# A causal convolution and a SiLU block on one core: the output weights' combinations on VectorE, and another order for the first blocks

## The chip, the cores and the metric

The kernel runs on one core of a Trainium2 chip. The metric is the device time of one execution in microseconds (us), lower is better. The profile and the trace come from one profiled execution; the runs' times come from executions of their own.

## The reference

What is computed, cut to what matters (all in float32):

```python
# x: (8, 4096, 192), weight: (8, 7), w_in: (192, 2048), w_out: (2048, 192)
w = exp(weight - max(weight, axis=-1)); w = w / (sum(w, axis=-1) + 1e-9)
x_pad = concatenate([zeros(B, 6, D), x], axis=1)
y[b, s, c] = sum over k of w[head(c), k] * x_pad[b, s + k, c]      # causal, 7 taps, 24 channels per head
h = y.reshape(32768, 192) @ w_in
g = h * (1 / (1 + exp(-h)))
out = g @ w_out
```

## The kernel before

**Work in blocks.** The 32768 tokens are cut into 32 blocks of 1024, and a block into two halves of 512. Channels are cut into 3 pieces of 64, the 2048 hidden units into 4 groups of 4 x 128. For each block the kernel loads x (SP's queue, line 289), transposes it (DVE, line 548), convolves it (first tap on ACT, line 579; six taps on DVE, line 582), copies pieces of the result to slots (DMAs on SP's queue, line 599), multiplies up to h (TensorE, called PE), takes SiLU (ACT), and multiplies down (PE) to the output, which is transposed (DVE, line 838) and stored (SP's queue, line 848).

**Fewer products.** From block 1 on, the up and down multiplications are written as bilinear schemes with fewer products. The up products of a block are 20 per group, 80 in all (line 656, two matmul records each). They take combinations of the convolved pieces (the *windows*, DVE, line 607) and combinations of the weights w_in, which are made once, in place, by `combine`: groups 0 and 1 on POOL, groups 2 and 3 on VectorE (DVE). The down multiplication takes sums of g (DVE, line 711) and combinations of w_out, made once by `combine_out`, in the tiles wx and, in place, wo. Block 0 is multiplied plainly, both ways: up at line 634, down at line 765. So wo may be combined only once block 0's plain down steps have read it, group by group.

**The order is written out by hand.** Every engine works through its own instructions in program order, and the program order of the loop is a list of tokens. `step(b, token)` (line 865) issues one token. A prefix says which block is meant: none is b, `-` is b-1, `=` is b-2, `+` is b+1. START (line 91) is run once with b = 2 and covers block 0's plain down steps, blocks 1 and 2, and block 3 up to its last up products and about half its output slots; PLAN (line 65) is then run for b = 3, 4, ... and begins with the rest of block b. The tokens that matter here:

- `ld.k`: four loads of x for the next block (SP's queue); `i.k`: the transpose of that piece; `ha.0`: the six columns ahead of the block
- `v.ki`: tap i of piece k, for the next block; `v.k0` is on ACT and `v.k1` to `v.k6` on DVE, each adding to the one before it. With `=` they make block 1's
- `sp.n`: one copy of a convolved piece to a slot (SP's queue), a piece's as soon as its six taps are in; `w.n`: a window. `w.3` and `w.4` need `sp.2`, `sp.3`, `sp.5` and `sp.6`, and `w.5` needs `w.4` and `sp.1`
- `Pn.g`: an up product of group g. The first, `P7.0`, reads window 4; `P1` and `P8` read window 5. `k12.0` copies a bank on DVE before `P2.0` may add to it. Other names with h, i, j, k, u or S are copies, sums and SiLU between products, on DVE and ACT
- `t.jk`: a sum of g for group j (DVE); `Di.je`: an output slot's four column-tiled matmuls (line 746). D2.30 needs t.30 and t.31, D5.30 needs t.33
- `M`, `z`, `y`, `x`: the merge of the output slots; `o.n`: a transpose of the merged output (DVE); `st.n`: its stores (SP's queue)
- `dp.n`: one of 48 plain down steps of block 0 (four matmul records at line 765), group j's last one being dp.11, dp.23, dp.35 and dp.47; `cp.n`: its copies out (ACT, line 783)
- `go.n`: half of the combination of w_in for groups 2 and 3, on DVE: go.0 and go.1 (7 and 6 operations) for one half of the rows, go.2 and go.3 (8 and 7) for the other, all of 64 x 256

SP's queue is also in program order: a store that waits for its transpose holds back the loads behind it.

**What the change touches.** `combine_out(j)` (line 488) makes four tensor_tensor operations of 128 x 192 (2 x 96 columns) for group j, through `comb` (line 467) on POOL. It is called for all four groups from the generator `down_plain` (line 755), at its end, right after the last plain step is issued (lines 777 to 779). POOL's earlier work is in its queue ahead of it: the combination of w_in for groups 0 and 1. DVE's work before the loop is the rounding of the weights (`rounded`, line 393).

Of the kernel before, what the change touches and what calls it, by code (L numbers as in the profile page):

```python
# [17 lines left out]
def kernel(  # L18
# [29 lines left out]
    NJ = NM // 2  # L48
# [43 lines left out]
        "=dp.0 =dp.1 =dp.2 =dp.3 =dp.4 =dp.5 =dp.6 =dp.7 =dp.8 =dp.9 =dp.10 =dp.11 =dp.12 =dp.13 "  # L92
        "=dp.14 =dp.15 =dp.16 =dp.17 =dp.18 =dp.19 =dp.20 =dp.21 =dp.22 =dp.23 =dp.24 =dp.25 "
        "=dp.26 =dp.27 =dp.28 =dp.29 =dp.30 =dp.31 =dp.32 =dp.33 =dp.34 =dp.35 =dp.36 =dp.37 "
        "=v.00 =dp.38 -ld.2 =v.01 =dp.39 =v.10 =dp.40 =dp.41 =v.11 =v.20 -ld.1 =v.02 =v.21 =v.03 "
        "=dp.42 =v.12 =dp.43 =v.04 =v.22 =v.13 =v.05 =v.23 =v.24 =dp.44 =v.06 =sp.0 =sp.3 =v.14 "
        "=v.25 =v.15 =sp.2 =dp.45 =v.26 =sp.7 =sp.10 =v.16 =sp.8 =go.2 =go.0 =sp.6 =sp.4 =sp.9 "
        "=w.0 =sp.1 =w.1 =w.2 =dp.46 =sp.5 =w.3 =w.4 -P7.0 =w.5 -P1.0 =cp.0 -P7.1 =cp.1 -P1.1 "
        "=dp.47 -h15.0 =go.1 -k12.1 -P8.0 -h15.1 -P2.1 -P8.1 -k12.0 -P2.0 -h17.1 =cp.2 =go.3 "
        "-P17.1 -u4.0 -P5.0 -P18.1 -k8.0 -j4.0 -ld.0 -h17.0 -u4.1 -P5.1 -S19.1 -j4.1 -k5.0 -i.2 "  # L100
        "-P18.0 =o.2 -P11.0 -u10.0 -P17.0 -P6.0 -P16.0 -k8.1 -P3.0 -P10.0 -P11.1 -h18.0 -i15_f.0 "
        "-P0.0 -P6.1 -u6.0 -P19.0 -k5.1 -S19.0 -P9.0 -j6.0 -P16.1 -k9.0 -P3.1 -u10.1 -P10.1 "
        "-P13.0 -S14.0 -i15_f.1 -u6.1 -P7.2 -h18.1 -S20.0 -P4.0 -j6.1 -P0.1 -P9.1 -P19.1 -k17.0 "
        "-k9.1 -P12.0 -j10.0 -P15.0 -S13.0 -P13.1 -i17_f.0 -S14.1 -i18_10.0 =o.0 -P7.3 -h15.2 "
        "-P4.1 -h15.3 -P8.2 -k17.1 -j10.1 -P1.2 -S20.1 -S13.1 -P14.0 -u4.2 -P12.1 -P8.3 -P1.3 "
        "-i15_11.0 -i17_f.1 -k12.2 -P15.1 -h17.2 -S16.0 -P5.2 -P17.2 -k12.3 -u4.3 -P2.2 -i18_10.1 "
        "-P18.2 -P2.3 -P14.1 -j4.2 -k8.2 =o.1 -P5.3 -i.0 -h17.3 -S15.0 -P17.3 -S19.2 -P11.2 "
        "-P18.3 -k5.2 -P3.2 =st.0 -P16.2 -i15_11.1 -j4.3 -S18.0 -S16.1 -k5.3 -P6.2 -u10.2 -u6.2 "
        "-S19.3 -h18.2 -k8.3 -P16.3 -P3.3 -h18.3 -P10.2 -P9.2 -P0.2 -P6.3 -P19.2 -t.00 -j6.2 "
        "-P11.3 -i15_f.2 -S17.0 -i.1 -u6.3 -k9.2 =st.1 -j6.3 -P19.3 -u10.3 -S14.2 -S20.2 -ha.0 "  # L110
        "-t.01 -P4.2 -k9.3 -P0.3 -P13.2 -S13.2 -t.03 -P10.3 -P13.3 -k17.2 -i15_f.3 -P4.3 -P15.2 "
        "-k17.3 -P9.3 -j10.2 -P15.3 -D0.01 -S13.3 -S14.3 -i18_10.2 -D4.00 -j10.3 -P14.2 -S16.2 "
        "-P12.3 -v.20 -i18_10.3 -P14.3 -ze.0 -P12.2 -S15.1 -t.02 -D4.01 =st.2 -i15_11.2 -D1.11 "
        "-i17_f.2 -S17.2 -D5.00 -D0.00 -D5.01 -D3.00 -D3.01 -i15_11.3 -v.21 -v.10 -S20.3 -v.22 "
        "-S17.1 -t.10 -D2.01 -v.00 -S18.1 -t.11 -t.13 -D0.20 -D2.11 -D2.00 -t.12 -D1.00 -D4.10 "
        "-i17_f.3 -D4.11 -D0.10 -D5.10 -D1.21 -S15.2 -D0.11 -D2.10 -v.23 -D0.21 -S18.2 -D5.11 "
        "-S17.3 -v.11 -D3.10 -S16.3 -D3.11 -D1.20 -S18.3 -t.20 -v.01 -D1.01 -D1.30 -t.21 -v.12 "
        "-D0.30 -v.02 -t.22 -D1.10 -S15.3 -D2.21 -D0.31 -D2.20 -t.23 -D3.20 -D4.20 -D4.21 -v.24 "
        "-v.13 -v.25 -t.30 -v.26 -v.14 -t.31 -sp.7 -D2.31 -D1.31 -y0.0 -z1.0 -v.03 -sp.9 -sp.8 "
        "-D2.30 -v.15 -y2.0 -v.04 -v.16 -D3.21 -v.05 -v.06 -D5.20 -t.33 -t.32 -D5.31 -D5.21 "  # L120
        "-sp.10 -y1.0 -D5.30 -D3.31 -sp.6 -D3.30 -sp.4 -D4.31 -D4.30 -w.0 -sp.2 -sp.0 -sp.5 -w.2 "
        "-sp.1 -w.1 -M1.0 -sp.3 -x0.0 -x2.2 -x2.1 -w.3 -w.4 -x2.0 P7.0 -w.5 -x1.0 ld.1 h15.0 P1.1 "
        "P7.1 -M3.0 P1.0 -x2.3 h15.1 k12.1 h17.1 P8.0 k12.0 u4.0 P2.1 P8.1 P2.0 P17.1 u4.1 -M2.0 "
        "P5.0 P18.1 P5.1 -M4.0 j4.0 -M5.0 k5.0 P16.0 P3.0 k8.0 h17.0 h18.0 S19.1 P18.0 P6.0 P17.0 "
        "u6.0 -M6.0 P11.0 P0.0 k8.1 j6.0 P9.0 P19.0 P11.1 S19.0 u10.0 S14.0 j4.1 P10.0 P6.1 k5.1 "
        "-o.0 P3.1 S20.0 k9.0 P16.1 u10.1 u6.1 -o.1 h18.1 -M7.0 P13.0 P7.2 P4.0 ld.2 P10.1 P9.1 "
        "P0.1 i15_f.0 j6.1 h15.2 i15_f.1 k17.0 P12.0 P19.1 j10.0 -o.2 S13.0 k9.1 P13.1 i17_f.0 "
        "P15.0 S20.1 P4.1 P7.3 S14.1 k17.1 S17.0 P1.2 i18_10.0 j10.1 h15.3 P8.2 S13.1 i.1 P12.1 "
        "P14.0 P1.3 u4.2 P8.3 P5.2 k12.2 P15.1 i15_11.0 P2.2 h17.2 P18.2 -st.0 S16.0 i17_f.1 u4.3 "
        "k12.3 P5.3 P17.2 S15.0 k8.2 i18_10.1 h17.3 -st.1 P11.2 j4.2 P14.1 S19.2 j4.3 P2.3 P18.3 "  # L130
        "ld.0 k5.2 P3.2 P17.3 i15_11.1 u10.2 i.0 u6.2 S18.0 S16.1 P6.2 k5.3 P16.2 P3.3 j6.2 S19.3 "
        "k8.3 P10.2 h18.2 P9.2 P16.3 P11.3 i15_f.2 P19.2 P6.3 P0.2 u6.3 -st.2 k9.2 h18.3 P13.2 "
        "S17.1 S14.2 S20.2 t.00 u10.3 P19.3 j6.3 P4.2 P10.3 -o.3 i.2 t.01 -st.3 ha.0 k9.3 k17.2 "
        "P13.3 S13.2 k17.3 P0.3 P15.2 P9.3 P4.3 t.03 S20.3 P15.3 D1.31 D1.11 D1.01 j10.2 v.00 "
        "S18.1 i15_f.3 S14.3 v.20 j10.3 P12.3 i18_10.2 i18_10.3 P14.2 P12.2 P14.3 ze.0 t.02 v.10 "
        "v.01 D1.21 i17_f.3 S15.1 D5.01 D4.00 D2.01 S16.2 t.10 S18.2 D4.01 D2.00 D5.00 i17_f.2 "
        "t.11 D2.10 D0.00 D0.10 v.11 v.02 D2.11 i15_11.2 S15.2 t.13 v.12 D3.00 D3.01 D1.10 t.12 "
        "D4.11 i15_11.3 D0.21 D5.11 v.03 S17.3 D4.10 D3.11 S18.3 D1.30 S17.2 v.04 D0.01 D0.11 "
        "D1.20 t.20 D0.20 v.21 S15.3 D5.10 t.21 v.22 t.22 v.13 D3.10 D2.21 t.23 v.14 D4.21 D2.20 "
        "D5.21 D0.31 D3.21 v.05 v.23 S13.3 v.24 D4.20 D3.20 S16.3 D1.00 D0.30 z1.0 D5.20 v.15 "  # L140
        "v.25 v.16 v.06 v.26 sp.5 t.30 t.31 D2.30 D2.31 sp.1 t.33 t.32 D3.30 D5.30 D5.31 D4.31 "
        "D3.31 D4.30 sp.8 sp.4 y2.0 sp.7 sp.9 w.0 y0.0 sp.2 sp.0 sp.10 x2.1 w.2 sp.6 w.3 w.1 sp.3 "
        "y1.0 w.4 x0.0 +P7.0 M1.0 x1.0 x2.3 +h15.0 w.5 +P1.1 x2.0 +P7.1 +h15.1 +P1.0 +P8.0 M2.0 "
        "M3.0 +k12.1 +h17.1 +u4.0 +P2.1 +k12.0 x2.2 +P8.1 +P2.0 M4.0 +j4.0 +P18.1 +P5.0 +P17.1 "
        "M5.0 +u4.1 +P5.1 +k5.0 +h17.0 +P16.0 +P3.0 +P18.0 +k8.0 +P6.0 M6.0 +u6.0 +j4.1 +h18.0 "
        "+S19.1 +k8.1 +P17.0 +j6.0 M7.0 +P11.0 +P0.0 +S19.0 +P9.0 o.1 +P19.0 +P11.1 +u10.1 +k5.1 "
        "+P16.1 +P3.1 +u10.0 +S20.0 +k9.0 +P10.0 +i15_f.0 +h18.1 +P6.1 +P10.1 +u6.1 +P13.0 +P19.1 "
        "+P4.0 +P0.1 +S14.0 +k17.0 +S13.0 +P9.1 +j6.1 +P7.2 +P12.0 +k9.1 +i15_f.1 +j10.0 +P15.0 "
        "+P1.2 +S20.1 +P7.3 +h15.2 +S14.1 +i17_f.0 +P13.1 +P8.2 +P4.1 +k12.2 +k17.1 +i18_10.0 "
        "+h15.3 +j10.1 +P14.0 +S17.0 +S13.1 +u4.2 +P2.2 +P8.3 +P12.1 +i15_11.0 +P15.1 +h17.2 "  # L150
        "+i17_f.1 +P5.2 +i18_10.1 +u4.3 +P17.2 +P1.3 +S15.0 +k12.3 +S16.0 +P18.2 +P5.3 +P14.1 "
        "+j4.3 +k8.2 +h17.3 st.1 +P11.2 +P18.3 +P2.3 +S19.2 +S16.1 +P17.3 +j4.2 +i15_11.1 +k5.2 "
        "+P6.2 +u10.2 +P16.2 +k5.3 +P3.2 +P16.3 +u6.2 +S19.3 +P3.3 +j6.2 +P10.2 +k8.3 +h18.2 "
        "+P6.3 +i15_f.2 +u6.3 +P19.2 +h18.3 +j6.3 +P9.2 +S18.0 +P0.2 +P11.3 +P0.3 +k9.2 +P4.2 "
        "+P19.3 +S14.2 +S20.2 +P13.2 +u10.3 +k9.3 +P10.3 +P13.3 +S13.2 +t.00 +S18.1 +S20.3 +k17.2 "
        "+D1.00 +P15.2 +P4.3 +t.01 +i15_f.3 +k17.3 +P15.3 +P12.3 +D1.11 +D0.00 +D1.31 +D0.01 "
        "+t.03 +j10.3 +S13.3 +t.02 o.2 +D4.01 +i17_f.3 +D3.00 +j10.2 +i18_10.3 +P9.3 +i18_10.2 "
        "+P14.2 +P12.2 +P14.3 +D1.21 +i17_f.2 +D3.01 +S15.1 +S17.2 o.3 +D4.00 +ze.0 +S17.1 +D5.00 "
        "+S16.2 +D0.20 +S17.3 +i15_11.2 +D5.01 +D2.01 +D2.00 +i15_11.3 st.3 +D1.01 o.0 st.0 "
        "+S18.2 +S15.2 +D1.10 +S15.3 +t.10 +D0.10 +D1.20 +D0.31 +t.11 st.2 +D0.11 +S18.3 +t.13 "  # L160
        "+D2.10 +D4.10 +D5.11 +D2.11 +D1.30 +D0.30 +t.20 +t.21 +D2.21 +D2.20 +D0.21 +S14.3 +D4.11 "
        "+S16.3"
# [592 lines left out]
    def down_plain(b):  # L755

        cmbs[b] = [xpool.tile([P, 4, TB], F32, tag="cmb", name="cmb")]
        for j in range(NJ):
            for a in range(2):
                for e in range(2):  # L760
                    for k in range(NK):
# [12 lines left out]
                        if (a, e, k) == (1, 1, NK - 1):  # L774
                            for c in range(2):
                                del gs[b, j, c]
                            if j == NJ - 1:
                                for c in range(NJ):
                                    combine_out(c)
# [344 lines left out]
```

## Time and profile before

| | us |
|---|---|
| median of 3 runs (lowest to highest) | 2352.57 (2352.14 to 2353.25) |
| the profiled execution's own time | 2355.45 |
| span of its trace | 2353.7 |
| PE busy in the span | 2329.8 (99%) |
| DVE busy | 2180.5 (93%) |
| ACT busy | 1329.0 (56%) |
| POOL busy | 70.0 (3%) |
| DMA, the largest queue (q1), share of 16 engines over the span | 23.1% |

A row of a group in the profile reads: line, engine, operation, output tile <- input tiles, shape, count, then busy time and the mean duration of one in ns, then the idle time of that engine just before such instructions, and what ended it. "L257" is a helper's line that issues every operation of the pinned vector, scalar and POOL engines that has no line of its own. A row of the chain reads: start, duration, and the engine, tile and line whose work the end of the program goes back to. A row of a table of stretches reads: the stretch, its length, and each engine's busy time with the number of instructions, then the granted clock of PE, the DMA engines' busy share and GB/s. PE's records overlap, so its busy time hides small gaps.

### The profile page before, as it was taken

Reading aid. Unit: us, or ns where it says so; the run is one execution under the profiler, and the core shown is the slowest. Engines: PE = TensorE matmul, PEld = TensorE weight load, DVE = VectorE, ACT = ScalarE, POOL = GpSimd, SP = SyncE. Lnnn points to the kernel's source line nnn. Section 1 sums busy time; section 2 is a strip of 40 time slices with the busy share of each in tenths; the row PEclk is TensorE's granted clock in tenths of the full one; section 3 lists DMA queues with packets and bytes.
Section 4 is the critical chain, followed back from the end, with each engine's and each line's share of the span. In section 5 each row is a group of like instructions: output and inputs, shape, how many; then the busy total and the mean of one; then the engine's idle time right before and its main releaser. Section 6 shows DMA issues by size and latency. Waiting matters only on the chain.

```text
span 2353.7 us, 43777 instructions
## 1 busy us (share of the span) xinstructions
PE 2329.8 (99%) x17382; PEld 919.1 (39%) x17382; DVE 2180.5 (93%) x3029; ACT 1329.0 (56%) x2523; POOL 70.0 (3%) x100
## 2 busy tenths in 40 slices
PE   9999989999999999999999999999999999999998
PEld 4344423344333443333443333433334433334433
DVE  8999889999999999999999999999999999999996
ACT  5256535666555765556665457654557655566654
POOL 4500000000000000000000000000000000000000
PEclk9999989999999999999999999999999999999999
DMA  7212122122122222121221221221222221212211
GB/s 157 52 31 36 29 53 49 28 52 52 33 46 45 35 52 48 34 49 30 51 52 37 42 51 30 53 51 30 49 34 47 52 43 40 49 28 52 53 32 23
DMA packets 451245, 106.55 MB, mean 45 GB/s; under 512 B 423584, under 2 KB 428704, under 8 KB 451040
## 3 DMA queue, kind: packets, MB, share of 16 engines
q1 hardware_dynamic: 447392, 101.78, 23.1%
q8 instruction: 136, 2.23, 0.4%
q0 software_dynamic: 448, 1.58, 0.3%
q10 hardware_dynamic: 3200, 0.39, 0.1%
q14 instruction: 69, 0.57, 0.1%
HBM read 31.46 MB, written 25.17 MB: 24 GB/s over the span
## 4 chain that ended last, share of the span: by engine, by line
PE 93%; DVE 2%; SPq 0%; issue 0%; ACT 0%; DMA 0%; ACTq 0%; DVEq 0%
PE ps L746 47%; PE ps L656 46%; DVE nat L582 1%; DVE t L711 0%; SPq L289 0%; DVE w_own L257 0%; DVE g L694 0%; SPq L848 0%; DVE w_other L257 0%; DMA nat<-in_x_dram 0%; DVE ps L694 0%; PE ps L765 0%; DVE u L678 0%; ACT g L691 0%; DVE cmb L257 0%
## 5 line engine op out<-in xcount | busy, mean ns | idle before, releaser
L656 PE MATMUL ps<-win,w_own 64*128 64x512 f32 x1488 | 660.5, 599 | 5.5 <-DVE win L607 5.5
L746 PE MATMUL ps<-g,wo 128*32 128x512 f32 x2976 | 663.6, 593 | 0.0
L746 PE MATMUL ps<-t,wo 128*32 128x512 f32 (+1 forms) x4528 | 512.1, 448 | 0.0
L746 PE MATMUL ps<-t,wx 128*32 128x512 f32 x2976 | 487.5, 595 | 10.9 <-DVE t L711 10.9
L656 PE MATMUL ps<-dup,w_own 64*128 64x512 f32 x1240 | 494.9, 594 | 0.2 <-ACT ps L689 0.2
L691 ACT ACTIVATE g<-ps 128x512 f32<-128x512 f32 x620 | 366.5, 599 | 189.8 <-DVE g L694 112.3
L656 PE MATMUL ps<-dup,w_other 64*128 64x512 f32 x1240 | 457.6, 595 | 0.2 <-ACT ps L689 0.2
L656 PE MATMUL ps<-win,w_other 64*128 64x512 f32 x992 | 446.9, 597 | 0.0
L694 DVE TENSOR_TENSOR g<-g,ps 128x512 f32<-128x512 f32 x496 | 331.6, 684 | 60.9 <-PE ps L656 40.1
L582 DVE SCALAR_TENSOR_TENSOR nat<-xt,turned,nat 128x512 f32<-128x512 f32 x558 | 383.1, 753 | 3.2 <-ACT nat L579 1.1
L811 ACT COPY yx<-ps 32x512 f32<-32x512 f32 x150 | 84.3, 579 | 508.8 <-PE ps L746 507.1
L656 PEld LDWEIGHTS ps<-win,w_own 64*128 64x128 f32 x1488 | 246.6, 186 | 213.7 <-issue 127.5
L711 DVE TENSOR_TENSOR t<-g,t 128x1024 f32<-128x1024 f32 x248 | 302.7, 1221 | 19.4 <-PE ps L746 9.5
L711 DVE TENSOR_TENSOR t<-g 128x1024 f32<-128x1024 f32 x248 | 300.9, 1214 | 12.7 <-PE ps L746 12.7
L746 PEld LDWEIGHTS ps<-t,wo 128*32 128x32 f32 x4528 | 175.7, 110 | 247.9 <-issue 189.4
L694 DVE TENSOR_TENSOR ps<-u,ps 128x512 f32<-128x512 f32 x372 | 255.2, 687 | 13.3 <-PE ps L656 6.1
L656 PEld LDWEIGHTS ps<-dup,w_own 64*128 64x128 f32 x1240 | 195.5, 186 | 144.3 <-issue 78.2
L746 PE MATMUL ps<-g,wx 128*32 128x512 f32 x1488 | 245.6, 592 | 0.0
L691 ACT ACTIVATE g<-g 128x512 f32<-128x512 f32 x372 | 220.5, 625 | 32.5 <-DVE g L694 29.2
L689 ACT ACTIVATE ps<-ps 128x512 f32<-128x512 f32 x372 | 214.7, 584 | 38.1 <-DVE ps L694 19.9
L746 PEld LDWEIGHTS ps<-g,wo 128*32 128x32 f32 x2976 | 172.9, 110 | 146.4 <-issue 145.4
L656 PEld LDWEIGHTS ps<-dup,w_other 64*128 64x128 f32 x1240 | 167.2, 186 | 132.8 <-ACT ps L689 50.7
(102 smaller groups left out, 1838.3 us busy)
## 6 DMA issues: line engine op xcount, KB each, us to landing
dup<-nat SPq DMA_DIRECT2D x221, 128.0 KB, 2.3
nat<-in_x_dram SPq DMA_DIRECT2D x382, 64.0 KB, 2.4
out_dram<-t SPq DMA_DIRECT2D x372, 64.0 KB, 2.0
win<-nat SPq DMA_DIRECT2D x124, 128.0 KB, 2.4
raw<-in_moe_w_out_dram SPq DMA_DIRECT2D x8, 384.0 KB, 3.6
raw<-in_moe_w_in_dram SPq DMA_DIRECT2D x12, 192.0 KB, 5.0
w_other<-w_own POOLq DMA_DIRECT2D x8, 192.0 KB, 5.0
raw<-in_moe_w_in_dram SPq DMA_DIRECT2D x6, 128.0 KB, 3.1
```

What stands on the lines that cost most here:

```text
L582: nc.vector.scalar_tensor_tensor(out=dst, in0=src, scalar=tap, in1=dst, op0=ALU.mult, op1=ALU.add)
L656: nc.tensor.matmul(at(b, "bank", to, g), raw(g, w, e), rows(slot_of(b, x_), e), start=first, stop=True, skip_group_check=True,)
L689: pin(nc.scalar.activation(seen[to], seen[u], AF.Copy, scale=-1.0))
L691: pin(nc.scalar.activation(seen[to], seen[u], AF.Silu, scale=float(sign)))
L694: pin(nc.vector.tensor_tensor(seen[to], seen[u], seen[v], op=op))
L711: pin(nc.vector.tensor_tensor(t[i // 2][:, i % 2, :], u, v, op=ALU.subtract))
L746: nc.tensor.matmul(acc[SQ * q : SQ * q + SQ, to], lhs[:, e, SQ * k : SQ * k + SQ], rhs[:, e, ts(q, TB // 4) if i == 5 else to], start=firs ...
L811: pin(nc.scalar.copy(to, acc(3 * (name[0] == "x") + k)[n:P, :]))
```

## The change

`combine_out` issues its four operations on DVE instead of POOL, and is no longer called from the end of `down_plain`. A new token, `co.j`, calls it for one group. START becomes another order of the same tokens, with the four `=co` added; PLAN is unchanged. No other instruction is added or left out.

```diff
     START = (
-        "=dp.0 =dp.1 =dp.2 =dp.3 =dp.4 =dp.5 =dp.6 =dp.7 =dp.8 =dp.9 =dp.10 =dp.11 =dp.12 =dp.13 "
...
-        "=v.00 =dp.38 -ld.2 =v.01 =dp.39 =v.10 =dp.40 =dp.41 =v.11 =v.20 -ld.1 =v.02 =v.21 =v.03 "
-        "=dp.42 =v.12 =dp.43 =v.04 =v.22 =v.13 =v.05 =v.23 =v.24 =dp.44 =v.06 =sp.0 =sp.3 =v.14 "
-        "=v.25 =v.15 =sp.2 =dp.45 =v.26 =sp.7 =sp.10 =v.16 =sp.8 =go.2 =go.0 =sp.6 =sp.4 =sp.9 "
-        "=w.0 =sp.1 =w.1 =w.2 =dp.46 =sp.5 =w.3 =w.4 -P7.0 =w.5 -P1.0 =cp.0 -P7.1 =cp.1 -P1.1 "
-        "=dp.47 -h15.0 =go.1 -k12.1 -P8.0 -h15.1 -P2.1 -P8.1 -k12.0 -P2.0 -h17.1 =cp.2 =go.3 "
...
+        "=v.10 =v.20 =v.11 =v.21 =v.12 =v.22 =v.13 =v.00 =v.23 =v.01 =v.24 =v.02 =dp.0 =v.14 "
+        "=v.03 =v.25 =v.04 =v.26 =sp.7 =dp.1 =sp.10 =v.05 =v.15 =v.06 =sp.8 =v.16 =sp.9 =go.2 "
+        "=sp.4 =sp.2 =w.0 =dp.2 =sp.0 =w.1 =sp.5 =w.2 =go.3 =w.3 =dp.3 =sp.6 =dp.4 =dp.5 =sp.3 "
+        "-ld.0 =dp.6 =dp.7 =dp.8 =w.4 =dp.9 =dp.10 =dp.11 =co.0 =dp.12 =dp.13 =sp.1 =dp.14 =dp.15 "
...
+        "=dp.40 =dp.41 =dp.42 =go.0 =dp.43 =dp.44 =dp.45 =dp.46 =cp.0 -P7.0 =dp.47 -h15.0 -P8.0 "
+        "-P1.1 =cp.1 -P1.0 -u4.0 -P5.0 -P7.1 -k12.0 -k12.1 -k8.0 =o.1 -P2.0 -j4.0 =cp.2 =co.3 "
...
     def combine_out(j):
...
-        comb(x_[0], a_(1, 0), a_(1, 1), ALU.add)
-        comb(x_[1], x_[0], a_(0, 0), ALU.subtract)
-        comb(x_[2], a_(0, 1), x_[1], ALU.subtract)
-        comb(a_(1, 0), a_(0, 0), a_(1, 0), ALU.subtract)
+        vec.tensor_tensor(x_[0], a_(1, 0), a_(1, 1), op=ALU.add)
+        vec.tensor_tensor(x_[1], x_[0], a_(0, 0), op=ALU.subtract)
+        vec.tensor_tensor(x_[2], a_(0, 1), x_[1], op=ALU.subtract)
+        vec.tensor_tensor(a_(1, 0), a_(0, 0), a_(1, 0), op=ALU.subtract)
...
                         if (a, e, k) == (1, 1, NK - 1):
                             for c in range(2):
                                 del gs[b, j, c]
-                            if j == NJ - 1:
-                                for c in range(NJ):
-                                    combine_out(c)
...
+        elif name == "co":
+            combine_out(digits[0])
```

In block 1's part of the new list, the rest of DVE's early work stands so: `=go.1` between `-u10.1` and `-i15_f.1`, `=co.1` behind `-j6.1`, `=co.2` behind `-i15_f.0`. In the part for block 3, its stores and turned outputs now stand among its up products; these are the lines of before, then of after, that hold block 2's four `o` and four `st`:

```diff
-        "+S19.1 +k8.1 +P17.0 +j6.0 M7.0 +P11.0 +P0.0 +S19.0 +P9.0 o.1 +P19.0 +P11.1 +u10.1 +k5.1 "
...
-        "+j4.3 +k8.2 +h17.3 st.1 +P11.2 +P18.3 +P2.3 +S19.2 +S16.1 +P17.3 +j4.2 +i15_11.1 +k5.2 "
...
-        "+t.03 +j10.3 +S13.3 +t.02 o.2 +D4.01 +i17_f.3 +D3.00 +j10.2 +i18_10.3 +P9.3 +i18_10.2 "
-        "+P14.2 +P12.2 +P14.3 +D1.21 +i17_f.2 +D3.01 +S15.1 +S17.2 o.3 +D4.00 +ze.0 +S17.1 +D5.00 "
-        "+S16.2 +D0.20 +S17.3 +i15_11.2 +D5.01 +D2.01 +D2.00 +i15_11.3 st.3 +D1.01 o.0 st.0 "
-        "+S18.2 +S15.2 +D1.10 +S15.3 +t.10 +D0.10 +D1.20 +D0.31 +t.11 st.2 +D0.11 +S18.3 +t.13 "
...
+        "+P10.0 +S19.0 +j6.0 M7.0 +k5.1 +P6.1 o.2 +S14.0 +P16.1 +k9.0 +P3.1 +u10.1 +P10.1 +S20.0 "
+        "+P13.0 o.1 +P7.2 +h18.1 +u6.1 o.0 +i15_f.0 +k17.0 +P4.0 +i15_f.1 +h15.2 +j6.1 +P0.1 "
...
+        "+h17.2 +P8.3 +j10.1 +P5.2 +P15.1 o.3 +i15_11.0 +P2.2 +i17_f.1 +u4.3 +k12.3 +P17.2 +P2.3 "
+        "+P18.2 +i18_10.1 +S16.0 +k8.2 +P11.2 +P14.1 +P5.3 +j4.2 st.0 +S15.0 +t.00 +i15_11.1 "
+        "+h17.3 +S19.2 +P17.3 st.2 +k5.2 +P3.2 +P18.3 +j4.3 +P6.2 +P16.2 +S16.1 +u10.2 +k5.3 "
+        "+P3.3 +P16.3 +u6.2 +S19.3 +P9.2 +P10.2 +j6.2 +h18.2 +P0.2 +k8.3 st.1 +h18.3 +t.02 +P11.3 "
+        "+P6.3 +S14.2 +k9.2 +P19.2 +u6.3 +P19.3 +i15_f.2 +P13.2 +P4.2 +u10.3 +S20.2 +j6.3 +k9.3 "
+        "st.3 +P10.3 +P13.3 +t.01 +k17.2 +S17.0 +P0.3 +i15_f.3 +P4.3 +k17.3 +P15.2 +P15.3 +P12.2 "
...
```

## The prediction

> **What bounds the kernel now.** I read the page's groups first, for which engine is never idle and what it waited for when it was; then the chain of waits in order of time, for where the idle time lies; then a table of stretches; then the instructions around the two places found.
>
> From the page, the groups of TensorE (PE) with idle time worth naming:
>
> ```profile
> L656 PE MATMUL ps<-win,w_own 64*128 64x512 f32 x1488 | 660.5, 599 | 5.5 <-DVE win L607 5.5
> ...
> L746 PE MATMUL ps<-t,wx 128*32 128x512 f32 x2976 | 487.5, 595 | 10.9 <-DVE t L711 10.9
> ```
>
> PE waits 5.5 us once for a window and 10.9 us once for a sum of g, both made by VectorE (DVE), and for nearly nothing else in 2353.7 us. The chain says when; its pieces that start a block's up products are
>
> ```profile
> 106.56 4.41 PE ps L656 x8
> ...
> 182.67 33.37 PE ps L656 x151
> ...
> 254.31 4.63 PE ps L656 x18
> ...
> 332.65 8.45 PE ps L746 x64
> 341.10 33.29 PE ps L656 x151
> ...
> 412.66 33.30 PE ps L656 x151
> ```
>
> Blocks 1 to 5 begin there: they take 76.1, 71.6, 86.8 and 71.6 us. From 341.10 on every block takes 71.56, which is PE's own work: 80 products of 0.44 (160 matmuls in 33.3 + 1.9), 40 output slots of 0.86, 8 short ones of 0.22, in all 71.3. So the steady loop can't give anything, and it is not changed. START, which ends inside block 3, holds all there is to gain. By stretches (columns: PE, PE weight loads, DVE, ACT, POOL busy; granted clock; DMA share; GB/s):
>
> ```profile
> 100.00:120.00 20.00, 14.52 (x51) 6.85 (x49) 16.81 (x36) 7.86 (x14) 0.00 (x0) 0.83 0.19 38
> ...
> 320.00:340.00 20.00, 9.10 (x76) 2.54 (x68) 19.65 (x28) 3.08 (x7) 0.50 (x1) 0.66 0.31 73
> ```
>
> Each stop is paid twice: idle, then the granted clock is low. The trace's clock records put it at half from 105.94 to 112.77 and from 324.40 to 338.05.
>
> **Stop 1, at 101 to 106.6.** PE ends the last plain down step but one at 101.08 and needs window 4. DVE was never idle before it: it ran v until 96.68, go.2 and go.0 until 103.1, then the windows until 106.4. The 18 v (rows of line 582 alone):
>
> ```profile
> 80.28:92.28 12.00, 11.96 (x12) 1.00 0.00 0
> 93.29:96.70 3.41, 3.39 (x6) 1.00 0.45 106
> 317.87:330.13 12.26, 12.19 (x18) 0.77 0.10 23
> ```
>
> and POOL in the first two stretches:
>
> ```profile
> 80.28:92.28 12.00, 11.53 (x13) 1.00 0.00 0
> 93.29:96.70 3.41, 0.00 (x0) 1.00 0.45 106
> ```
>
> While POOL works, a v starts every 1.00 us; once POOL stops, every 0.66, as in block 3 (18 in 12.26). POOL's work there is combine_out.
>
> **Stop 2, at 321.8 to 332.65.** SP's queue, then DVE's, in block 3:
>
> ```profile
> 298.26 6.03 SPq L848 DMA_DIRECT2D out_dram<-t  x9
> 304.33 7.57 SPq L289 DMA_DIRECT2D nat<-in_x_dram  x12
> ...
> ```
>
> ```profile
> 313.86 0.71 DVE L548 STREAM_TRANSPOSE xt<-nat 128x512 f32<-128x512 f32 x1 [1.39 <-DMA nat<-in_x_dram]
> ...
> 317.87 12.26 DVE L582 SCALAR_TENSOR_TENSOR nat<-xt,turned,nat 128x512 f32<-128x512 f32 x18
> ...
> 331.37 1.23 DVE L711 TENSOR_TENSOR t<-g,t 128x1024 f32<-128x1024 f32 x1
> ```
>
> Block 2's turned outputs (o.3, o.0) stand late in START, so nine stores issue at 298.3, the twelve loads behind them end at 311.9, 57.6 us into the block, and DVE's three transposes wait, with the v, t.30 and t.31 behind them. PE's D2.30 needs t.31. In block 4 the twelve loads issue at 363.15 (22 us into the block) and nothing waits.
>
> **The change, part by part.** *POOL loses combine_out (16 operations, 77.6 to 92.8 and 96.9).* The last two rounding operations before the v, 1.34 and 1.23 us, fall to the 0.95 that the same kind took at 37.6 to 40.5 without POOL's arithmetic: 0.7. Thirteen v at 0.66 for 1.00: 4.4. The new first v (v.11) needs ACT's v.10, which three ACT operations from 76.05 cover. So the v end at 96.68 - 5.1 = 91.6. The Trainium skill (SBUF — State Buffer, section "SBUF: two separate sides") says VectorE with two SBUF inputs and GpSimd lock a port pair for a whole instruction; the pace of 1.00, and not 0.66 + 0.7 (POOL's shortest row), shows slowing, not full turns; the sum takes the measured pace.
>
> *The order up to window 4.* Before it DVE has 15 go operations (go.2, go.3 in place of go.2, go.0) and five windows, as now, 9.4 to 9.7 us: window 4 ends at 101.1. The shares it copies are issued as each third of the v ends, the last needed one (sp.3) at about 94.7 behind nine others of 0.6, and lands 2.4 later, well before. P7.0 then starts at 101.25 instead of 106.56: **-5.3**, with PE's own 101.08 late next.
>
> *What DVE owes after it.* co.0 before window 5, go.0 before k12.0, go.1 and co.1 to co.3 among the products. No row has combine_out on DVE. Below: 0.29 (tensor_scalar, 64x256). Above: 0.69 (128x512). I take 0.36, a little under the 0.42 of a 64x256 tensor_tensor, as 192 columns are fewer: 1.45 per co, 5.8 in all (4.6 to 11.0). P7.0 and the last plain step cover 1.3; co.0 and window 5 take 2.1, so PE waits 0.65 for P8.0. Five products (2.2) later P2.0 needs k12.0, behind go.0's 7 x 0.42: a wait of 1.4. From there DVE is full: k12.0 to w.4 of block 1 are 67.4 us of DVE against 72.2 of PE, DVE starting 4.7 behind, and P15.0, P14.0, P13.2 have margins of 0.1 to 0.4; I allow 1.0. Sum 3.0. Today's block 1 loses 76.1 - 71.56 - 0.86 (the last plain step) = 3.7, mostly half clock: **-0.7**. The co operations' own waits (plain steps 11, 23, 35, 47) end by 102.6 and hold nothing up.
>
> *Block 2* (71.64) keeps its work and slack: 0. Its loads and stores issue between its products.
>
> *Block 3.* The four o of block 2 and its stores now stand ahead of the block's first D, as PLAN has them, so the loads should issue as in block 4. DVE has 65.4 us of work there in 71.56. Late next would be t.33, 0.5 us before PE's D5.30 in block 4. 86.8 - 71.56 = 15.2; I leave 0.2: **-15.0**.
>
> Sum 21.0. The profiled execution took 2355.45 (span 2353.7), so 2334.4; the median of the runs is 2.88 under it: **2331.6**. Without any loss in blocks 1 to 3 it would be 24.0 to 24.4 and 2328.2 to 2328.6. DVE's first term needs the prologue untouched, which it is.
>
> **Rivals.**
> *Half clock again (2335.0).* The second drop came 2.65 us after PE's idle began (321.75 to 324.40), and the half-clock times are 6.83 and twice 6.83. My 0.65 and 1.4 fall in two such windows (99.12 to 112.77). If little waits are enough, 6.83 us run at half speed: +3.4. No gap up to 0.76 between matmul starts did it at full clock; the point lies between. The Trainium skill (TensorE: Matmul & The Clock Gate, part 1) puts it at an idle window of some 3.4 us; by that no wait of mine trips it, but the 2.65 here is already under it.
>
> *Late DVE (2336 to 2342).* If the transposes of block 4 come over 45.6 us into block 3, or block 1's backlog grows by over 2 us, each further us is PE's; from 2.65 on the clock adds 3.4. Five late: +8.4, 2340. One whole stop that stays is +15.0, 2346.6.
>
> *No loss at all (2328.5).* The backlog's margins hold and co costs less.
>
> *DVE's sum is the bound, slower (2358.6).* If PE at 332.65 waits for DVE's amount of work and not its order, the end moves by what DVE gains and gets: -5.1 and +11.0 at 0.69 per operation, +5.9. It decides for slower when an operation costs over 0.61. Against: DVE is idle some 29 us between 100 and 320 (16.81, 15.92, 14.56, 14.66 of 20).
>
> *It does nothing (2352.6):* at 0.36 the same sum is +0.7; also against the idle time.
>
> **Chances.** Forecast, 2329.5 to 2334: 0.50. No loss: 0.10. Half clock: 0.15. Late DVE 0.14, a third of it over 2340. One stop stays 0.05. Slower 0.04. Nothing 0.02. Range 2328.0 to 2340.0 leaves out about 0.18. Over 0.2% (4.7 us, about what a measurement can tell from no change) faster: 0.94; same 0.02; slower 0.04.
>
> **What would show it.** The v in 12 us, ending near 91.6; POOL idle after 77.5; P7.0 near 101.3; PE's waits for DVE of 0.65 and 1.4 there, and no half clock between; twelve loads in block 3 some 22 us into it; blocks of 75, 71.6 and 71.6. It is wrong if a v still takes 1.00, if a co takes over 2.5, or if PE waits for t.31 again.

## The result, and the profile after

The changed kernel takes 2333.9 us, median of 4 runs (2333.65 to 2334.63); the kernel before, run beside it, 2352.85 (2352.14 to 2353.25). The ratio is 0.992, 95% interval 0.9903 to 0.9937. The forecast was 2331.6, range 2328.0 to 2340.0. The profiled execution took 2334.11, with a span of 2332.4 against 2353.7.

The page's groups with PE's idle time, as before: line, engine, tiles, shape, count | busy, mean ns | idle before, and what ended it.

```profile
L656 PE MATMUL ps<-win,w_own 64*128 64x512 f32 x1488 | 661.4, 598 | 0.8 <-DVE win L607 0.5
...
L746 PE MATMUL ps<-t,wx 128*32 128x512 f32 x2976 | 484.7, 592 | 0.0
```

The waits of 5.5 and 10.9 us are down to 0.8 and 0.0. The chain in order of time (start, duration, what):

```profile
106.22 31.17 PE ps L656 x138
...
175.67 33.87 PE ps L656 x151
...
247.81 34.05 PE ps L656 x150
...
320.12 33.29 PE ps L656 x151
...
391.68 33.29 PE ps L656 x151
```

Block 4 begins at 320.12 instead of 341.10: 20.98 us of the span's 21.3 were won before it. The clock records hold no half clock between 5.4 us and 2329.9; PE's last work ends at 2326.4.

The rows behind the two stops. The 18 v of block 1 (line 582 alone; stretch, length, DVE busy, then clock, DMA share and GB/s), and SP's queue and DVE in block 3:

```profile
79.41:91.41 12.00, 12.00 (x18) 1.00 0.10 23
```

```profile
260.57 8.28 SPq L845 DMA_DIRECT2D out_dram<-t  x12
268.89 6.37 SPq L289 DMA_DIRECT2D nat<-in_x_dram  x12
```

```profile
292.92 1.89 DVE L548 STREAM_TRANSPOSE xt<-nat 128x512 f32<-128x512 f32 x3
...
297.05 1.22 DVE L711 TENSOR_TENSOR t<-g 128x1024 f32<-128x1024 f32 x1
298.19 12.26 DVE L582 SCALAR_TENSOR_TENSOR nat<-xt,turned,nat 128x512 f32<-128x512 f32 x18
```

All v run at 0.66 us and end at 91.4; the twelve loads issue 21 us into block 3 (50 before), and the three transposes run without a wait.

### The profile page after: what moved, and what is told of

Same layout as the page of the kernel before. It is cut to its first block, busy times and chain, and to the rows that moved or that the text cites. A ratio compares the mean times of both kernels' runs of the same rounds, so it can differ in the third digit from the quotient of the medians.

```text
span 2332.4 us, 43764 instructions
## 1 busy us (share of the span) xinstructions
PE 2324.2 (100%) x17382; PEld 921.5 (40%) x17382; DVE 2178.5 (93%) x3045; ACT 1330.8 (57%) x2523; POOL 53.7 (2%) x84
## 2 busy tenths in 40 slices
DMA packets 451246, 106.55 MB, mean 46 GB/s; under 512 B 423585, under 2 KB 428705, under 8 KB 451041
## 4 chain that ended last, share of the span: by engine, by line
PE 95%; DVE 1%; SPq 0%; DMA 0%; issue 0%; ACT 0%; ACTq 0%
PE ps L746 48%; PE ps L656 47%; SPq L599 0%; DVE t L711 0%; DMA nat<-in_x_dram 0%; DVE win L607 0%; DVE u L678 0%; DVE w_other L257 0%; SPq L289 0%; DVE w_own L257 0%; DVE cmb L257 0%; DVE ps L694 0%; ACT u L257 0%; DVE g L694 0%; DVE wx L257 0%
## 5 line engine op out<-in xcount | busy, mean ns | idle before, releaser
L582 DVE SCALAR_TENSOR_TENSOR nat<-xt,turned,nat 128x512 f32<-128x512 f32 x558 | 378.2, 746 | 3.9 <-ACT nat L579 1.6
```

Of the source, the lines that this page charges most:

```text
L582: nc.vector.scalar_tensor_tensor(out=dst, in0=src, scalar=tap, in1=dst, op0=ALU.mult, op1=ALU.add)
```

## The experiments

Each was timed in runs of its own beside runs of the kernel before. "Starts" are those of the 1st, 161st, 321st and 481st matmul of line 656, that is of blocks 1 to 4, in the profiled execution; "blocks" are the differences. The medians of the kernel before range from 2352.85 to 2355.58, so rows with different ones are better compared by starts and blocks.

| kernel | median | before beside it | ratio, 95% interval | block 1 starts | blocks 1, 2, 3 |
|---|---|---|---|---|---|
| before | 2352.85 | | | 106.56 | 76.04, 71.64, 86.79 |
| after | 2333.90 | 2352.85 | 0.9903 to 0.9937 | 100.98 | 74.62, 72.14, 72.31 |
| e0_before | 2354.72 | 2354.41 | 0.9989 to 1.0008 | 106.78 | 75.34, 71.78, 86.66 |
| e1_pool | 2343.71 | 2354.41 | 0.9932 to 0.9965 | 106.45 | 77.61, 72.19, 72.46 |
| e2_dve_old | 2353.70 | 2354.41 | 0.9986 to 1.0004 | 101.46 | 80.03, 71.63, 85.74 |
| e12_pool_late | 2342.14 | 2355.58 | 0.9931 to 0.9956 | 105.67 | 77.18, 72.24, 72.40 |
| e5_go0_co0 | 2336.53 | 2353.48 | 0.9917 to 0.9942 | 101.07 | 77.65, 71.61, 72.23 |
| e7_go1_first | 2338.79 | 2355.58 | 0.9915 to 0.9942 | 101.36 | 77.97, 72.12, 72.54 |
| e9_oldnew | 2339.45 | 2353.48 | 0.9927 to 0.9954 | 106.35 | 75.05, 71.63, 72.94 |
| e10_newold | 2348.37 | 2353.48 | 0.9969 to 0.9987 | 100.87 | 74.62, 72.23, 85.98 |
| e3_stores | 2354.72 | 2354.41 | 0.9989 to 1.0008 | 106.55 | 75.54, 71.63, 86.55 |
| e11_stores_d | 2350.52 | 2353.48 | 0.9979 to 0.9997 | 106.50 | 76.03, 71.63, 83.50 |
| e13_d411 | 2348.16 | 2355.58 | 0.9955 to 0.9977 | 101.57 | 74.62, 71.95, 84.47 |
| e6_late | 2346.41 | 2355.58 | 0.9949 to 0.9976 | 101.04 | 74.62, 71.88, 83.78 |

In the diffs of START below a token stands on a line of its own.

### The kernel before, again

No edit.

> The kernel before, unchanged, profiled again. Its first profile (2355.45 us) lies 2.6 us over the median of its runs (2352.85), while the changed kernel's profile (2334.11) lies on its median: that is why the median moved by 18.95 and the spans by 21.3. Theory (phase of the clock): the two stops are the same in every run, and what differs is how long the clock stays at half after them, 6.83 and 13.65 us in the first profile; then this profile is some 2 to 3.5 us shorter, its first product still starts near 106.6 and its D2.30 still waits 10 to 11 us, and the half-clock records are shorter by 5 to 7 us in all. Rival (the stops themselves vary): the waits for DVE are shorter by 2 to 3 us and the half-clock records are as long as before.

Both stops are there again (6.3 and 10.9 us of idle, 5.5 and 10.9 in the first profile); the half-clock records are 6.83 and 10.24 instead of 6.83 and 13.65. This profile took 2356.25, so it is not shorter, and the expectation fails as it was put. What it shows is the spread: 35 runs of the kernel before on this chip, counted with this copy's, lie between 2352.65 and 2356.86; those at a granted clock of 0.995 (7) have a median of 2356.2, those at 0.996 (28) of 2354.2. So the clock after the stops takes part in the spread, and other things do too.

### The first stop: POOL, the order, and DVE's work in block 1

**combine_out back on POOL, at the new places.**

```diff
-        vec.tensor_tensor(x_[0], a_(1, 0), a_(1, 1), op=ALU.add)
+        pool.tensor_tensor(x_[0], a_(1, 0), a_(1, 1), op=ALU.add)
...
```

(the same for the other three operations)

> The new list, with combine_out's four operations per group back on POOL (still at the co tokens). Theory (POOL slows the v): the v start every 1.00 us again while POOL works, 12 to 14 of them, so window 4 ends 4 to 5 us later (105 to 106), P7.0 starts near 105.5, the half clock comes back for about 6.8 us; DVE is spared 5.7 us in block 1. Time 2333.9 + 4.5 + up to 3.4 - up to 1.5 = 2337 to 2341. Rival (the new order alone makes the v fast): the v keep 0.66 us and the time is 2332 to 2334.

Measured 2343.71, a little over the stated range, and the first stop is back: block 1 starts at 106.45, after 6.2 us of idle, with a half clock of 10.24. The place differs from what was expected. Only groups 0 and 1 reached the v (18 in 13.35 us instead of 12.00). POOL then waited for the plain steps until 96.0, and its other nine operations ran beside the windows and go.3:

```profile
97.73 2.96 DVE L607 TENSOR_TENSOR dup<-dup 128x512 f32<-128x512 f32 x3
...
101.35 0.81 DVE L257 TENSOR_TENSOR w_own<-w_own 64x256 f32<-64x256 f32 x1
102.08 0.81 DVE L257 TENSOR_TENSOR w_other<-w_other,w_own 64x256 f32<-64x256 f32 x1
```

Three windows take 2.96 for 1.89 in the changed kernel, a go operation 0.81 for 0.42. So the new order alone does not make DVE early; POOL delays any of these operations.

**combine_out on DVE in the old order.**

```diff
-        comb(x_[0], a_(1, 0), a_(1, 1), ALU.add)
+        vec.tensor_tensor(x_[0], a_(1, 0), a_(1, 1), op=ALU.add)
...
```

(again all four)

> The old list, with combine_out on DVE, all four groups at its old place, behind the last plain down step. Theory: the v run at 0.66 us, window 4 ends near 101 and P7.0 starts near 101.2 (5.3 earlier); then 16 operations of 0.355 us stand in front of go.1 and k12.1 on DVE, so PE waits some 5 to 6 us there and the half clock comes: block 1 gains 0 to 3 us in all. The second stop (10.9 us of idle before D2.30) stays, since the late stores stay. Time 2350 to 2353. Rival (the second stop is DVE's amount of work): block 3 ends later by up to 5.7 us, 2355 to 2358.

Measured 2353.70: the interval of the ratio holds 1. Block 1 starts at 101.46, 5.1 earlier, and gives it back: 80.03 for 76.04, with PE waiting behind the 16 operations.

```profile
PE ps L746 <- DVE t L711: 10.6, 1, 10.6
PE ps L656 <- DVE ps L678: 4.0, 1, 4.0
```

(Waits of PE: tile and line, for whom, us in total, times, longest.) The second stop stays at 10.6. That says little about DVE's sum, which has hardly changed: the 16 operations take 5.3 us (101.96 to 107.25), and DVE comes to window 4 5.1 earlier. The engine alone is worth nothing; the change needs the order.

**combine_out on POOL behind everything.**

```diff
 =dp.11
-=co.0
 =dp.12
...
 =co.3
+=co.0
+=co.1
+=co.2
 -h15.1
...
```

(co.1 and co.2 likewise taken from their places; operations on POOL as in e1_pool)

> The changed kernel's list with combine_out on POOL again, but all four groups behind the last plain down step (co.3 first, so POOL can't start before 102 us): DVE is spared 5.7 us in block 1 and the v stay undisturbed. Theory (POOL slows those DVE operations that read two SBUF tensors, like the v; block 1's sums, copies and products' operands read PSUM): block 1 takes 73.2 to 74.4 us instead of 74.6, time 2332.5 to 2333.7. Rival (POOL slows DVE whatever it reads, for the 13 to 15 us that 16 operations take): block 1 takes 76 to 79, time 2335.5 to 2338.

Measured 2342.14, over both ranges, but it is no test of block 1's operations: the premise was wrong. The first three operations of a group only read wo, so they need not wait for a plain step, and the fourth writes the half of wo that step 41 is the last to read. POOL ran its other 13 operations from 96.3 to 107, beside go.3 and the windows again:

```profile
99.92 0.82 DVE L257 TENSOR_TENSOR w_other<-w_other,w_own 64x256 f32<-64x256 f32 x1
100.66 0.81 DVE L257 TENSOR_TENSOR w_own<-w_other,w_own 64x256 f32<-64x256 f32 x1
...
103.56 0.96 DVE L607 TENSOR_TENSOR win<-dup,win 128x512 f32<-128x512 f32 x1
104.56 0.96 DVE L607 TENSOR_TENSOR win<-win 128x512 f32<-128x512 f32 x1
```

```profile
99.68 0.78 POOL L257 TENSOR_TENSOR wo<-wo 128x192 f32<-128x192 f32 x1
100.42 0.77 POOL L257 TENSOR_TENSOR wx<-wo 128x192 f32<-128x192 f32 x1
```

A go operation starts every 0.74 us (0.40 in the changed kernel), a window every 1.00 (0.73). With the v's 1.00 for 0.66, each of these DVE operations loses about 0.3 beside POOL, long or short. POOL keeps the same pace: it too starts an operation every 0.74 us beside the go, so one of DVE goes with one of POOL.

**What DVE owes in block 1, put off.**

```diff
 =w.4
...
-=co.0
...
 =w.5
...
 =dp.42
-=go.0
...
 -u10.1
+=go.0
 -P18.0
...
 =co.2
+=co.0
```

> The changed kernel with go.0 moved from in front of k12.0 to behind u10.1, and co.0 from in front of window 5 to behind co.2. Theory (in block 1 PE's small waits come from what DVE owes ahead of k12.0): P8.0's and P2.0's waits go, block 1 shrinks by 0.5 to 1.5 us; time 2332.4 to 2333.4. Rival (DVE is full in block 1, so what is put off is paid later): the waits move to later products or to block 2's windows, time 2333.7 to 2335.

Measured 2336.53, and block 4 starts at 322.56 for 320.05 in the changed kernel; the rival was right, and by more than it said. Without go.0 DVE has nothing to do between window 5 and k12.0:

```profile
105.13 1.90 DVE L678 COPY ps<-ps 128x512 f32<-128x512 f32 x3 [3.48 <-PE ps L656]
```

It idles 3.48 us for PE, and the same work then stands in front of later sums, for which PE waits: block 1 takes 77.65. In the changed kernel go.0 and co.0 fill that hole, and k12.0 starts at 105.48, 0.35 later than here.

**More of it ahead of k12.0.**

```diff
 =go.0
+=go.1
...
 -P18.0
-=go.1
 -u10.0
```

> The changed kernel with go.1 (2.3 us of DVE) moved in front of k12.0. PE's gap before P2.0 grows from 0.9 to about 3.2 us. DVE's amount of work stays. Theory (a wait of about 2.7 us or more can bring the half clock, as in the first profile's second stop): in some runs 3.4 us or more at half clock, 1.7 us or more each; time 2335.5 to 2339, with runs further apart than the changed kernel's. Rival (only a wait over 3.4 us does): no half clock, 2335 to 2336.3.

Measured 2338.79. The theory had the half clock in some runs only, with runs further apart; the four lie within 0.6 (2338.32 to 2338.92). PE waits 2.40 us before P2.0, and the half clock comes, for 3.41 us in the profile. The stretches on both sides of its start (length; PE, PE weight loads, DVE, ACT, POOL; clock; DMA share, GB/s):

```profile
106.16:109.57 3.41, 1.01 (x6) 0.55 (x5) 3.34 (x9) 0.86 (x2) 0.00 (x0) 1.00 0.00 0
109.57:112.99 3.42, 3.42 (x10) 2.58 (x9) 3.35 (x9) 1.88 (x4) 0.00 (x0) 0.50 0.03 5
```

The clock falls when PE has worked again for 0.85 us. Block 1 takes 3.35 longer.

### The second stop: which part of the order

**The old first part with the new block 3, and the other way about.** START is cut at block 3's first product: the tokens ahead of it from one list, the rest in the other list's order.

```diff
 x0.0
-+P7.0
+x2.0
 M1.0
-x1.0
++P7.0
 x2.3
-+h15.0
 w.5
+M3.0
...
```

> The old list up to block 3's first up product (with combine_out on POOL), the new list's order from there on. Theory (the two stops are independent and the second comes from block 3's order): the first stop stays (6 us of idle and 7 to 10 us at half clock), the wait before D2.30 goes, block 3 takes 71.6 to 72.5 us. Time 2354.4 - 14 to 16 = 2338.5 to 2340.5. Rival (DVE arrives at block 3 too late from the first part): a wait of 3 us or more stays before D2.30, 2344 or more.

> The new list up to block 3's first up product (with combine_out on DVE), the old list's order from there on. Theory: no first stop and no half clock at 105, P7.0 at 101; the second stop stays whole, 10 to 11 us of idle and some 10 us at half clock. Time 2333.9 + 14 to 16 = 2348 to 2350. Rival (an earlier DVE shortens the second stop): 2340 to 2346.

Measured 2339.45 and 2348.37, both as the theory had it, but for block 3 with the old first part (72.94, expected up to 72.5). The old first part keeps a wait of 6.1 for a window and loses the other; the new first part keeps 10.9 for t and loses the first. Block 4 starts at 341.03 with both old, 325.97 and 333.70 with one new, 320.05 with both: 15.1 and 7.3 alone, 21.0 together, 1.4 less than their sum.

**Block 2's outputs and stores alone, early in the old list.**

```diff
 +P6.1
+o.2
...
 +u6.1
+o.0
...
 +P15.1
+o.3
...
 +S16.1
+st.2
...
 +j4.2
+st.0
...
 +j6.3
+st.3
...
```

(taken from their old places)

> The old list and combine_out on POOL, with block 2's o.2, o.0, o.3 and st.0, st.2, st.3 alone moved to the places among block 3's up products that the new list gives them. Theory (the second stop comes from late stores in front of the loads on SP's queue): the twelve loads issue some 22 us into block 3 instead of 50, the wait before D2.30 goes, block 3 takes 71.6 to 73.5 us; the first stop stays. Time 2352.85 - 13 to 15 = 2337.5 to 2340. Rival (DVE's amount of work between 80 and 335 us sets the stop): 2349 to 2353.

Measured 2354.72, no gain: the theory falls, and with it the reason that the forecast gave for the second stop. The loads did issue early, at 277, and the transposes ran at 307 without a wait. But (line numbers are one less in this kernel):

```profile
311.09 1.23 DVE L710 TENSOR_TENSOR t<-g,t 128x1024 f32<-128x1024 f32 x1 [0.92 <-PE ps L745]
316.24 1.22 DVE L710 TENSOR_TENSOR t<-g 128x1024 f32<-128x1024 f32 x1 [3.92 <-PE ps L745]
317.39 12.26 DVE L581 SCALAR_TENSOR_TENSOR nat<-xt,turned,nat 128x512 f32<-128x512 f32 x18
```

The row at 316.24 is t.22. It waits for PE's output slots, and the v behind it start where they did before. DVE idles 3.92 us ahead of it, so the rival, DVE's amount of work, doesn't explain the stop either. t.22 writes a half tile of an earlier sum that D4.11 is the last to read, and the old list has D4.11 as the very last output slot of START, which ends 62 us into the block.

**D4.11 as well.**

```diff
 +D4.10
++D4.11
 +D5.11
...
 +S14.3
-+D4.11
 +S16.3
```

(on top of e3_stores)

> The old list with block 2's outputs and stores moved forward as in e3, and one output slot of block 3, D4.11, moved forward to stand behind D4.10 instead of last in START. In e3 the transposes were ready by 309 but t.22 sat until 316.2, waiting for PE. New theory: t.22 writes the half tile that D4.11 reads, so v and t.30 behind it on DVE wait for D4.11; with both moved, t.22 starts near 310.5, the v near 311.8 instead of 317.4, and the wait before D2.30 falls from 10.2 to 4 to 5 us. Time 2354.4 - 5 to 8 = 2346 to 2349. Rival (something else holds t.22, or DVE's amount of work does): 2352 to 2355.

Measured 2350.52: the right way, but half of it. The v start at 314.55 for 317.4, PE waits 7.0 for 10.2. t.23 now waits 1.77 for PE: D2.11, whose half tile it writes, had come 0.86 later by the slot put in front.

**D4.11 alone, late in the new list.** One token of the changed kernel moves:

```diff
 +t.13
-+D4.11
 +D5.11
...
 +D1.30
++D4.11
 +S14.3
```

> The changed kernel with one token moved: D4.11, an output slot of block 3, stands last in START instead of behind t.13. PE's work is the same. Theory (the other cause: t.22 writes what D4.11 reads): t.22 waits for PE until some 60 us into block 3, the v start near 309 instead of 298.2, PE waits 9 to 10.5 us before D2.30, plus 3 to 5 us for half clock. Time 2346 to 2349. Rival (t.22's wait in e3 had another reason): 2333.5 to 2335.

Measured 2348.16, as the theory had it:

```profile
296.54 1.22 DVE L711 TENSOR_TENSOR t<-g,t 128x1024 f32<-128x1024 f32 x1
309.49 1.23 DVE L711 TENSOR_TENSOR t<-g 128x1024 f32<-128x1024 f32 x1 [11.73 <-PE ps L746]
```

One output slot moved by 15 us, with no work added, makes t.22 wait 11.73 us and PE 10.2 us for t.31: nearly the whole second stop.

**The outputs and stores alone, late in the new list.**

```diff
 +t.03
+o.2
...
 +S17.1
+o.3
...
 +i15_11.3
+st.3
 +t.11
+st.2
...
 +D1.00
+o.0
+st.0
...
```

(taken from their new places)

> The changed kernel with block 2's o.2, o.3, o.0 and st.3, st.0, st.2 alone moved back to late places in block 3, as in the old list. Theory (two causes of the second stop, each enough by itself; this is the stores): the twelve loads issue some 46 us into block 3 instead of 21, the transposes end near 55 us into it, the v start 8 to 9 us later than in the changed kernel, and PE waits 7 to 8 us before D2.30, plus 2 to 5 us for half clock. Time 2343 to 2347. Rival (the stores never were a cause, as e3 would have it alone): 2333.5 to 2335.

Measured 2346.41, as the theory had it. The twelve loads issue at 295.3, 48 us into block 3, and

```profile
305.43 0.71 DVE L548 STREAM_TRANSPOSE xt<-nat 128x512 f32<-128x512 f32 x1 [2.00 <-DMA nat<-in_x_dram]
```

ends 58.6 us into it; PE waits 7.6. So the stores are a cause too, enough by themselves. (They also hold a tile that t.20 writes: at 296.94 DVE waits 2.04 us for their transfers.) In the old list both held DVE until about the same time, and taking the stores away showed nothing. D4.11 alone, moved in the old list, was not run.

## Why the prediction was right, step by step

**Block 1's start: right.** Forecast 101.25, measured 100.98; the v ended at 91.4 (91.6), window 4 at 100.83 (101.1). That the pace of 1.00 is POOL's was argued; e1_pool and e12_pool_late show it. The Trainium skill (SBUF — State Buffer, section "SBUF: two separate sides") lets the two engines take whole turns at a port pair when VectorE reads two SBUF inputs. Nearly all the operations slowed here do (a tensor_scalar with one input takes 0.57 for 0.29 in e12_pool_late). The forecast read slowing and not turns out of the pace of 1.00, because POOL's shortest row is 0.7. That does not follow: the two engines go one for one, and POOL's recorded time may hold waiting of its own. The runs show the price, about 0.3 us per operation; whether it comes from turns stays open.

**The price of a co operation: right.** Forecast 0.36 within 0.29 to 0.69; measured 0.33 to 0.36, and 1.3 per group from its start to the next operation's, 5.3 in all. Without POOL the v end 5.3 earlier (91.4 for 96.68). So the swap is even for DVE, as the forecast's sum of +0.7 nearly had it; the gain comes from the place, since the cost now lies behind window 4, where PE has products to do.

**Block 1's own loss: a little less.** Forecast 3.0 over PE's work (72.4), measured 74.62 - 72.4 = 2.2. Up to P2.0 it is 1.7 (5.2 us for 3.5 of work; forecast 2.05), behind it 0.5 for the 1.0 allowed.

```profile
103.01 1.99 PE L656 MATMUL ps<-win,w_other 64*128 64x512 f32 x6
...
106.22 0.69 PE L656 MATMUL ps<-win,w_own 64*128 64x512 f32 x1 [0.28 <-DVE ps L678]
```

The rows are P8.0 with the products behind it, and P2.0. The places differ. The wait for k12.0 was expected at 1.4; the start-to-start gap before P2.0 is 0.87, of which 0.43 is the product ahead of it. Put in its place: P7.0 and the last plain step take 2.03 instead of 1.3 (100.98 to 103.01): P7.0 runs alone, its two matmuls 0.50 apart, and 0.44 per product holds where two products run together. So window 5, done at 102.75, hardly makes P8.0 wait. P5.0 comes about 0.4 late, for which the forecast had no wait. That DVE is full was right; e5_go0_co0 shows it.

**Block 2: 0.5 too small.** 72.14 for 71.6. No run was made for the reason.

**Block 3: right in size, half in reason.** Forecast 71.8, measured 72.31. The step "the loads should issue as in block 4" came true, but it was not enough for the gain: e3_stores does that alone, and the wait stays at 10.2. The other half, D4.11 late in PE's own order and t.22 held by it, was not in the forecast; that the new list has D4.11 early as well was luck. It could be read from the kernel before, in PE's rows and in DVE's:

```profile
315.10 0.61 PE L746 MATMUL ps<-t,wx 128*32 128x512 f32 x3
```

```profile
315.60 1.21 DVE L711 TENSOR_TENSOR t<-g,t 128x1024 f32<-128x1024 f32 x1
316.73 1.22 DVE L711 TENSOR_TENSOR t<-g 128x1024 f32<-128x1024 f32 x1
```

The first row is the end of D4.11, at 315.71. t.22 is the last row: it follows directly on the operation ahead of it, so DVE, late from the transposes, sets its start. With the transposes early it would have waited for D4.11, and started at most 1.0 us earlier. Both were late at once, and the trace names the one that came last. The rival that DVE's sum sets the stop is out: in e13_d411 DVE works 68.8 us in block 3, in the changed kernel 68.1, and the stop is back.

**The median: 2.3 too low.** Block 4 starts 20.98 earlier, against the forecast's 21.0. That this is so close is in part luck: block 1's start and block 1 brought 0.3 and 0.7 more than forecast, blocks 2 and 3 each 0.5 less. The forecast then took 2.88 off for the way from the profiled execution to the median. That step failed: 2.88 was no offset of the profiler but one draw from the runs of the kernel before, which lie between 2352.1 and 2356.9, while the changed kernel's profiled execution is one of its four runs, 0.2 from their median.

**The half clock: not there.** The forecast knew of none up to 0.76 between matmul starts, and of one 2.65 us into an idle time. The changed kernel has gaps of 0.87 and 1.12 between matmul starts and no half clock. e7_go1_first has it at 2.99 between starts (2.40 of idle), e13_d411 not at 1.82 (101.57). The half-clock records of all runs, but for the last one at each kernel's end, last 3.41, 6.83, 10.24 or 13.65 us, multiples of 3.41. The Trainium skill (TensorE: Matmul & The Clock Gate, part 1) names a free-running window of 3413 ns, and an idle one as what throttles; the length agrees, but the window that throttled in e7_go1_first holds 1.01 us of PE's work.

In none of these kernels does block 4 start earlier than in the changed one.

## What to carry to other kernels

A wait has the last of several late things behind it, and taking that one away may show nothing: before a gain is counted, ask for each later operation of the stalled engine what it waits for, buffers that another engine must still read included. Two identical symptoms (loads late, a half tile still being read) were each enough here, and it took one kernel per cause, in the good order, to see both. And moving these 16 operations from GpSimd to VectorE changed VectorE's sum hardly at all, because its own operations had been slower beside GpSimd; what counts is which of VectorE's results is due next.

## What the hardware showed beside this

- The VectorE operations with two SBUF inputs lose about 0.3 us for each operation of GpSimd beside them, whether they take 0.40 by themselves (go, start to start 0.74), 0.66 (v, 1.00) or 0.73 (a window, 1.00), and GpSimd starts one operation for each of theirs. Three transposes with one SBUF input take 1.89 with GpSimd at work (70.35 in the kernel before) as without it (292.92 in the changed one).
- The clock can fall after PE is back at work: in e7_go1_first PE restarts at 108.72 and the half clock begins at 109.57.
